# A new order for every engine of a fused window-attention and rational-MLP kernel, with three output tiles

## The chip, the cores and the metric

The kernel runs on one core of a Trainium2 chip. The metric is the device time of one execution in microseconds (us); smaller is better. The five engines are named as in the profile: PE (TensorE, matrix products), DVE (VectorE), ACT (ScalarE), POOL (GpSimd, here mostly the issuer of loads) and SP (SyncE, the issuer of transposing transfers and stores). PEld is PE's weight load.

## The reference

A causal attention with a window of 128 positions and 4 sink positions, followed by an MLP whose activation is a rational function.

```python
scores = scale * np.matmul(q, k.transpose(0, 1, 3, 2))     # B, H, S, D = 4, 8, 768, 64
keep = is_sink | in_window                                  # 4 sinks, window 128
a = softmax of scores where keep
attn = np.matmul(a, v)
x = attn as (3072, 512)
h = x @ w_in                                                # 512 -> 2048
P = a[0] + a[1]*h + a[2]*h**2 + a[3]*h**3
Q = 1.0 + abs(b[0])*abs(h) + abs(b[1])*h**2
return (P / (Q + 1e-06)) @ w_out                            # 2048 -> 512
```

## The kernel before

The 3,072 rows are cut into 12 steps of 256 rows, three steps to a batch. A step s goes through these pieces, whose names are those of the kernel's table of work:

- loads of K, Q and V. K and Q of steps 0 to 3 are turned by PE (`turn_k0`, `turn_q0`, `turn_kc`, `turn_qc`) and copied out of PSUM by DVE or ACT (`place_kc`, `place_qc`); K and Q of later steps are turned by SP's transposing transfers (`turn_k`, `turn_q`). V of steps 0 to 2 is rearranged by PE (`turn_vc`) and copied out (`place_vc`).
- `scores` (4 per step, PE), `exps` (4 per step, ACT), `attend` (2 per step, PE), then on DVE a reciprocal of the row sums (`rec`, line 854) and the scaled copy `norm` (line 860) into the tile x_n.
- `turn_x` and `placed_x`: x is turned by PE and copied to xblk by DVE or ACT in steps 0 to 4, and turned by SP's transfers in steps 5 to 11.
- `gemm1` (4 per step, PE, line 910) and `copy_in` (ACT, line 917) give hb.
- The rational function, on tiles of 4,096 columns: `and` (absolute value, L931), a square (`sqa` on ACT L924, `sqd` on DVE L926), `den` (L935), `even` (L940), `odd` (L944), `odd_h` (L948), `num` (L951) on DVE; `ln` (L954) and `exp` (L959) on ACT, which form the reciprocal of the denominator; `gate` (L964) on DVE gives g. Step 0 is cut into four parts of 1,024 columns, the last step into parts of 1,280, 1,280, 1,024 and 512 columns.
- `gemm2` (PE, line 974), `copy_out` (ACT, line 990) into an output tile o_t, and `store` (SP).

The sinks' part of V has a path of its own at the start: the coefficients a and b and four rows of V arrive by small transfers, DVE splits and casts them (L627, L630, L533), PE spreads them over the partitions, and DVE writes v_sink (L555, `spread_vs`). `attend` needs v_sink.

The order is written out by hand as a list of piece numbers, ORDER. The kernel walks it once and emits each piece; every engine then runs its own pieces in the order of the list, in order, each waiting for what it needs. A negative number is a filler: matmuls on a constant tile `warm` (line 728) that feed nothing. A table ENGINE says which of DVE and ACT does some 30 copies, and a table BANK gives each product one of four pairs of PSUM banks (ps_h, ps_o, ps_m, ps_s); a pair is free again when the piece that empties it is done. POOL's copies of one element (`hold`, L507) read x_n or hb of a step, and so keep the loads behind them in POOL's queue back until that step's part is written.

```python
names = list(work)
for n in ORDER:
    if n < 0:
        spin(-n)
    elif work[names[n]].run:
        work[names[n]].run()
```

Of the kernel before, what the change touches and what calls it, by code (L numbers as in the profile page):

```python
# [1429 lines left out]
```

## Time and profile before

| | before |
|---|---|
| time, median of 3 runs | 232.76 us (232.26 to 233.08) |
| the profiled execution | 232.42 us, of which the span of its instructions is 230.7 us |
| PE busy | 215.9 us (94% of the span) |
| DVE busy | 211.1 us (91%) |
| ACT busy | 207.0 us (90%) |
| POOL busy | 97.3 us (42%) |
| bytes moved by DMA | 26.98 MB |

Busy time is the time in which an engine worked on an instruction; the rest of the span it waited. The span leaves out 1.72 us of the profiled execution that lie around the instructions. PE's busy time includes the fillers.

### The profile page before, as it was taken

What the parts mean: (1) busy time and instruction counts of PE and PEld (TensorE: products, weight loads), DVE (VectorE), ACT (ScalarE), POOL (GpSimd) and SP (SyncE); (2) the same over time, 40 slices, a digit from 0 to 9 for tenths busy, and PEclk for the clock granted to TensorE, in tenths of its full rate; (3) what the DMA queues carried; (4) which work ended last, traced back from release to release, by engine and by line L of the source; (5) the groups of instructions that cost most, each with busy time, mean ns of one, the idle gap of its engine ahead of it and who ended that gap; (6) DMA issues with size and microseconds to landing.
All of it is one profiled execution on the core that took longest, in us unless ns stands there. A gap on an engine that the chain in (4) does not pass through costs nothing.

```text
span 230.7 us, 7350 instructions
## 1 busy us (share of the span) xinstructions
PE 215.9 (94%) x3249; PEld 147.0 (64%) x3271; DVE 211.1 (91%) x251; ACT 207.0 (90%) x177; POOL 97.3 (42%) x126
## 2 busy tenths in 40 slices
PE   8768999989999999999999999999999999999992
PEld 2546777778747667667677577758856875544441
DVE  3595699879999999999999999999999999999991
ACT  2757889989997999999999999999999999799961
POOL 8914756967559499988199800000000000000000
PEclk9999999999999999999999999999999999999999
DMA  6999999999999999999969998230050200400152
GB/s 182 199 191 199 197 144 103 135 117 121 205 176 141 130 106 150 172 122 124 196 155 133 109 148 162 47 71 0 3 139 3 48 0 0 182 4 0 49 224 91
DMA packets 95237, 26.98 MB, mean 117 GB/s; under 512 B 85862, under 2 KB 92262, under 8 KB 95206
## 3 DMA queue, kind: packets, MB, share of 16 engines
q0 software_dynamic: 65024, 12.98, 90.4%
q1 hardware_dynamic: 28942, 12.75, 29.8%
q10 hardware_dynamic: 1240, 0.79, 1.1%
q8 instruction: 25, 0.41, 0.8%
q14 instruction: 6, 0.05, 0.1%
HBM read 27.30 MB, written 6.29 MB: 146 GB/s over the span
## 4 chain that ended last, share of the span: by engine, by line
PE 69%; DMA 19%; POOL 3%; DVE 3%; issue 2%; ACT 2%; SPq 0%; DVEq 0%; ACTq 0%
PE ps_s L974 13%; PE ps_h L974 11%; PE ps_o L910 9%; PE ps_m L974 9%; PE ps_m L910 7%; DMA w_out_sb<-in_moe_w_out_dram 6%; PE ps_s L910 5%; PE ps_h L910 5%; DMA stage_v<-in_v_dram 4%; DMA k_bf<-in_k_dram 3%; DMA stage_a<-in_k_dram 2%; POOL v L465 2%; DMA ab_row<-in_moe_a_dram 2%; PE ps_o L846 2%; DMA q_bf<-in_q_dram 1%
## 5 line engine op out<-in xcount | busy, mean ns | idle before, releaser
L910 PEld LDWEIGHTS <-w_in_sb 128*128 128x128 bf16 x768 | 73.8, 98 | 13.0 <-issue 1.2
L974 PEld LDWEIGHTS <-g 128*128 128x128 bf16 x386 | 36.4, 98 | 41.6 <-issue 1.4
L954 ACT ACTIVATE lnq<-den 128x4096 f32<-128x4096 bf16 (+3 forms) x18 | 44.6, 2482 | 1.5 <-DVE den L935 1.4
L959 ACT ACTIVATE den<-lnq 128x4096 bf16<-128x4096 f32 (+3 forms) x18 | 44.5, 2484 | 0.2
L465 POOL DMA_DIRECT2D v<-in_v_dram x48 | 35.0, 746 | 3.6 <-DMA w_out_sb<-in_moe_w_out_dram 1.5
L910 PE MATMUL ps_o<-xblk,w_in_sb 128*128 128x256 bf16 x304 | 36.3, 273 | 0.0
L974 PE MATMUL ps_s<-w_out_sb,g 128*128 128x512 bf16 x136 | 32.3, 379 | 0.8 <-issue 0.5
L974 PE MATMUL ps_h<-w_out_sb,g 128*128 128x512 bf16 x121 | 28.6, 379 | 0.9 <-issue 0.5
L964 DVE TENSOR_TENSOR g<-num,den 128x4096 bf16<-128x4096 bf16 (+3 forms) x18 | 28.3, 1572 | 0.3
L935 DVE TENSOR_TENSOR den<-den,sq 128x4096 bf16<-128x4096 bf16 (+3 forms) x18 | 28.3, 1570 | 0.2
L951 DVE TENSOR_TENSOR num<-num,sq 128x4096 bf16<-128x4096 bf16 (+3 forms) x18 | 28.3, 1572 | 0.1
L948 DVE TENSOR_TENSOR sq<-sq,hb 128x4096 bf16<-128x4096 bf16 (+3 forms) x18 | 28.2, 1569 | 0.1
L910 PE MATMUL ps_m<-xblk,w_in_sb 128*128 128x256 bf16 x208 | 24.9, 273 | 0.5 <-DMA w_in_sb<-in_moe_w_in_dram 0.5
L974 PE MATMUL ps_m<-w_out_sb,g 128*128 128x512 bf16 x90 | 21.6, 379 | 0.6 <-issue 0.5
L917 ACT ACTIVATE hb<-ps_o 128x1024 bf16<-128x1024 f32 x19 | 19.5, 1029 | 2.1 <-PE ps_o L910 1.9
L924 ACT ACTIVATE sq<-hb 128x1024 bf16<-128x1024 bf16 (+3 forms) x15 | 20.0, 1341 | 0.1
L427 POOL DMA_DIRECT2D q_bf<-in_q_dram x15 | 16.7, 1111 | 6.0 <-DMA w_out_sb<-in_moe_w_out_dram 2.6
L910 PE MATMUL ps_s<-xblk,w_in_sb 128*128 128x256 bf16 x160 | 19.1, 273 | 0.0
L940 DVE TENSOR_SCALAR num<-sq,acoef 128x4096 bf16<-128x4096 bf16 (+3 forms) x18 | 18.3, 1023 | 0.3
L944 DVE TENSOR_SCALAR sq<-sq,acoef 128x4096 bf16<-128x4096 bf16 (+3 forms) x18 | 18.4, 1021 | 0.3
L507 POOL COPY seen<-x_n 1x1 bf16<-1x1 bf16 x8 | 9.7, 1225 | 17.4 <-DVE x_n L860 17.4
L926 DVE TENSOR_TENSOR sq<-hb 128x2048 bf16<-128x2048 bf16 (+2 forms) x13 | 16.8, 1295 | 0.1
(154 smaller groups left out, 321.5 us busy)
## 6 DMA issues: line engine op xcount, KB each, us to landing
out_dram<-o_t SPq DMA_DIRECT2D x11, 512.0 KB, 3.6
w_in_sb<-in_moe_w_in_dram POOLq DMA_DIRECT2D x4, 512.0 KB, 10.8
k_bf<-in_k_dram POOLq DMA_DIRECT2D x16, 128.0 KB, 6.6
w_out_sb<-in_moe_w_out_dram POOLq DMA_DIRECT2D x4, 512.0 KB, 11.7
q_bf<-in_q_dram POOLq DMA_DIRECT2D x15, 128.0 KB, 5.4
v<-in_v_dram POOLq DMA_DIRECT2D x24, 64.0 KB, 6.3
stage_v<-in_v_dram POOLq DMA_DIRECT2D x3, 256.0 KB, 9.6
v<-in_v_dram POOLq DMA_DIRECT2D x24, 32.0 KB, 5.7
```

Source lines behind the costliest of these rows:

```text
L465: nc.gpsimd.dma_start(out=v_fix[b % 2][half(r), g * NHF:(g + steps) * NHF, hl, 0:D], in_=v[b, h, g * TS:(g + steps) * TS, :].rearrange("(j ...
L910: nc.tensor.matmul(ps[:, n, :], lhsT=w_in_all[:, c, fc * P:(fc + 1) * P], rhs=xblk[m][:, c, :], start=(c == 0), stop=(c == NDMC - 1))
L917: nc.scalar.activation(out=hb[m][:, j * GW:(j + 1) * GW], in_=ps_h.pop((m, j)).rearrange("p n c -> p (n c)"), func=AF.Copy)
L924: nc.scalar.activation(out=sq[m][:, c], in_=hb[m][:, c], func=AF.Square)
L935: nc.vector.tensor_tensor(out=den[m][:, c], in0=den[m][:, c], in1=sq[m][:, c], op=ALU.add)
L944: nc.vector.tensor_scalar(out=sq[m][:, c], in0=sq[m][:, c], scalar1=a3, scalar2=a1, op0=ALU.mult, op1=ALU.add)
L948: nc.vector.tensor_tensor(out=sq[m][:, c], in0=sq[m][:, c], in1=hb[m][:, c], op=ALU.mult)
L951: nc.vector.tensor_tensor(out=num[m][:, c], in0=num[m][:, c], in1=sq[m][:, c], op=ALU.add)
L954: nc.scalar.activation(out=lnq_fix[:, c], in_=den[m][:, c], func=AF.Ln, scale=qsc_reg, bias=1.000001)
L959: nc.scalar.activation(out=den[m][:, c], in_=lnq_fix[:, c], func=AF.Exp, scale=-1.0)
L964: nc.vector.tensor_tensor(out=g_of[m][:, c], in0=num[m][:, c], in1=den[m][:, c], op=ALU.mult)
L974: nc.tensor.matmul(ps_out[own][:, tt, cols], lhsT=g_of[m][:, co:co + P], rhs=w_out_all[:, fc, cols], start=(fc == 0), stop=(fc == NFFC - 1 ...
```

## The change

The list ORDER is replaced by another one, and with it the tables ENGINE and BANK. No piece is added or taken away, except that a filler in the middle of the list (211: five matmuls) is gone and the one at the start becomes longer by one matmul of 512 columns (154 becomes 258). The output tiles o_t are three instead of two, and `copy_out` of step m waits for the store of step m-3 instead of m-2. The staging tile of the sinks' rows of V, stage_s, becomes a part of the staging tile stage_b. The short description of the change also names K of step 1 as first load; in POOL's queue the first three loads are, before and after, V of step 0, Q of step 1 and K of step 1. The next two change places (K of step 2 now ahead of Q of step 3).

In ENGINE eight copies go from ACT to DVE, and ten from DVE to ACT: `cast_q0` 1, both `cast_k0`, `place_k0` 0, `k_sink` 0 and 2, `place_vc` 0, `place_kc` 3, `placed_x` 2,0 and 4,1 to ACT; `cast_q0` 0, `place_k0` 1, `place_qc` 0,1 and 3,0, `k_sink` 1 and 3, `place_vc` 2 and `placed_x` 0,0 to DVE.

```diff
 ORDER = [
-    118, 2, 3, 0, -154, 108, 107, 129, 109, 117, 4, 119, 113, 116, 120, 121, 122, 1, 125, 143,
...
+    118, -258, 2, 3, 0, 108, 107, 109, 5, 119, 113, 4, 117, 120, 121, 122, 15, 1, 125, 143, 144,
...
-    ENGINE = {('cast_q0', 1): 'DVE',
-               ('place_kc', 3, None): 'DVE',
+    ENGINE = {('cast_q0', 1): 'ACT',
+               ('place_kc', 3, None): 'ACT',
...
-               ('place_vc', 0): 'DVE',
...
+               ('place_vc', 0): 'ACT',
...
-    BANK = {('attend', 0, 0): 'ps_s',
+    BANK = {('attend', 0, 0): 'ps_m',
...
-    o_sb = ctx.enter_context(tc.tile_pool(name="o_sb", bufs=2))
+    o_sb = ctx.enter_context(tc.tile_pool(name="o_sb", bufs=3))
...
-    stage_s = const_pool.tile([SR, B, D], FP32, name="stage_s")
+    stage_s = stage_b[0:SR, NQ0 * H * D:NQ0 * H * D + B * D].rearrange("p (b d) -> p b d", b=B)
...
-                      ends + [("store", m - 2, 0) if m >= 2 else None],
+                      ends + [("store", m - 3, 0) if m >= 3 else None],
...
```

What the new list does to the rows of an engine is shown at three places on DVE. The first is DVE's start, from the last sinks (v_sink, three rows) to the first instruction of the rational function (L931). qT, kT and xblk are the turned Q, K and x. Before:

```order
L555 TENSOR_TENSOR v_sink<-ps_o,ind 128x8x64 x3
L854 RECIPROCAL rec<-ps_s 128x8
L860 SCALAR_TENSOR_TENSOR x_n<-ps_s,ratio,rec 128x512
L679 COPY xblk<-ps_s 128x2x256
L679 COPY qT_101<-ps_m 128x4x128
L854 RECIPROCAL rec<-ps_h 128x8
L860 SCALAR_TENSOR_TENSOR x_n<-ps_h,ratio,rec 128x512
L370 MEMSET k_sink_104 128x80
L931 TENSOR_SCALAR den<-hb 128x512
```

And in the change, from the second `norm` of step 0 to the same instruction:

```order
L860 SCALAR_TENSOR_TENSOR x_n<-ps_s,ratio,rec 128x512
L679 COPY qT_102<-ps_o 128x2x384
L679 COPY xblk<-ps_s 128x2x256
L679 COPY xblk<-ps_o 128x2x256
L606 COPY cpow<-ratio 128x1
L607 TENSOR_TENSOR qsc<-bpos,ratio 128x1
L608 TENSOR_SCALAR cpow<-cpow,ratio 128x2
L610 TENSOR_TENSOR acoef<-ab_bc,cpow 128x4
L679 COPY qT_101<-ps_h 128x4x128
L931 TENSOR_SCALAR den<-hb 128x512
```

Half of step 3's Q (qT_102, 768 columns) and both halves of step 0's x are now DVE's, and L931 stands ahead of the first `norm` of step 1 instead of behind it.

The second place is DVE at the attention of step 3, whose two `rec` and `norm` stand together. Before:

```order
L860 SCALAR_TENSOR_TENSOR x_n<-ps_m,ratio,rec 128x512
L948 TENSOR_TENSOR sq<-sq,hb 128x1024
L745 TENSOR_TENSOR e_1_94<-e_1_94,sink_edge 128x4
L679 COPY xblk<-ps_m 128x4x128
L948 TENSOR_TENSOR sq<-sq,hb 128x1024
L854 RECIPROCAL rec<-ps_h 128x8
L854 RECIPROCAL rec<-ps_m 128x8
L860 SCALAR_TENSOR_TENSOR x_n<-ps_h,ratio,rec 128x512
L860 SCALAR_TENSOR_TENSOR x_n<-ps_m,ratio,rec 128x512
```

The change, from the same `norm` of step 2 on:

```order
L860 SCALAR_TENSOR_TENSOR x_n<-ps_m,ratio,rec 128x512
L948 TENSOR_TENSOR sq<-sq,hb 128x1024
L944 TENSOR_SCALAR sq<-sq,acoef 128x1024
L948 TENSOR_TENSOR sq<-sq,hb 128x1024
L951 TENSOR_TENSOR num<-num,sq 128x1024
L679 COPY xblk<-ps_h 128x4x128
L964 TENSOR_TENSOR g<-num,den 128x1024
L854 RECIPROCAL rec<-ps_o 128x8
L854 RECIPROCAL rec<-ps_s 128x8
L860 SCALAR_TENSOR_TENSOR x_n<-ps_s,ratio,rec 128x512
```

Ahead of the two `rec` there are now more pieces of step 0's rational function (`num`, `gate`), and one copy to xblk of step 2 instead of two, the other being ACT's.

The third place is DVE at the attention of step 5. Before, its two `rec` (ps_m and ps_h) stand behind `odd` and `odd_h` of step 2:

```order
L944 TENSOR_SCALAR sq<-sq,acoef 128x4096
L931 TENSOR_SCALAR den<-hb 128x2048
L854 RECIPROCAL rec<-ps_o 128x8
L860 SCALAR_TENSOR_TENSOR x_n<-ps_o,ratio,rec 128x512
L948 TENSOR_TENSOR sq<-sq,hb 128x4096
L854 RECIPROCAL rec<-ps_m 128x8
L679 COPY xblk<-ps_o 128x4x128
L854 RECIPROCAL rec<-ps_h 128x8
```

In the change both stand ahead of these two (the `rec` and `norm` of step 4, ps_o, are further up):

```order
L940 TENSOR_SCALAR num<-sq,acoef 128x4096
L931 TENSOR_SCALAR den<-hb 128x2048
L854 RECIPROCAL rec<-ps_h 128x8
L854 RECIPROCAL rec<-ps_s 128x8
L944 TENSOR_SCALAR sq<-sq,acoef 128x4096
L860 SCALAR_TENSOR_TENSOR x_n<-ps_h,ratio,rec 128x512
L948 TENSOR_TENSOR sq<-sq,hb 128x4096
L860 SCALAR_TENSOR_TENSOR x_n<-ps_s,ratio,rec 128x512
```

The two `rec` of step 5 moved up past `odd` (L944) and `odd_h` (L948) of step 2.

## Rows read from the trace of the kernel before

**Rows 1.** The page: busy time, then busy tenths and clock in 40 slices.

```profile
PE 215.9 (94%) x3249; PEld 147.0 (64%) x3271; DVE 211.1 (91%) x251; ACT 207.0 (90%) x177; POOL 97.3 (42%) x126
...
DVE  3595699879999999999999999999999999999991
...
PEclk9999999999999999999999999999999999999999
```

**Rows 2.** Waits of DVE: us in total, times, longest us.

```profile
DVE ab_part L627 <- DMA ab_row<-in_moe_a_dram: 1.5, 1, 1.5
...
DVE rec L854 <- PE ps_o L846: 0.4, 1, 0.4
```

**Rows 3.** Busy us of PE, PEld, DVE, ACT, POOL in three stretches, then granted clock.

```profile
10.00:15.00 5.00, 3.09 (x95) 2.29 (x84) 3.71 (x10) 3.31 (x5) 2.58 (x4) 1.00 1.73 186
...
40.00:50.00 10.00, 9.15 (x249) 7.59 (x247) 8.08 (x18) 9.23 (x11) 9.37 (x16) 1.00 2.12 116
...
190.00:200.00 10.00, 9.95 (x62) 5.90 (x62) 10.00 (x6) 9.40 (x7) 0.00 (x0) 1.00 0.08 32
```

**Rows 4.** DVE in order of time at the end: start us, us, what.

```profile
225.15 0.42 DVE L964 TENSOR_TENSOR g<-num,den 128x512 bf16<-128x512 bf16 x1
227.18 0.43 DVE L679 COPY o_t<-ps_o 128x256 f32<-128x256 f32 x1 [1.60 <-ACT o_t L677]
```

**Rows 5.** Groups of DVE's copies by shape: count, busy us, mean ns, idle before.

```profile
L679 DVE COPY kT<-ps_m 128x1024 bf16<-128x1024 bf16 x1 | 1.2, 1225 | 0.2 <-PE ps_m L661 0.2
...
L679 DVE CAST early<-stage_a 128x512 bf16<-128x512 f32 x2 | 1.0, 484 | 0.4 <-DMA stage_a<-in_k_dram 0.4
...
L679 DVE COPY xblk<-ps_m 128x512 bf16<-128x512 bf16 x2 | 0.8, 424 | 0.4 <-PE ps_m L885 0.2
...
L679 DVE COPY kT<-ps_m 128x512 bf16<-128x512 bf16 x1 | 0.7, 671 | 0.0
```

**Rows 6.** DVE in order of time, 0 to 45 us.

```profile
12.13 1.21 DVE L679 CAST v<-ps_o 128x1024 bf16<-128x1024 f32 x1
...
33.13 0.68 DVE L951 TENSOR_TENSOR num<-num,sq 128x1024 bf16<-128x1024 bf16 x1
```

**Rows 7.** PE in order of time, 0 to 45 us.

```profile
1.13 5.42 PE L728 MATMUL ps_h<-warm 128*128 128x512 bf16 x15 [1.13 <-DVE warm L1099]
...
13.39 0.64 PE L661 MATMUL ps_o<-ident,stage_d 128*64 128x128 bf16 x16 [1.18 <-DVE v L679]
...
16.56 0.77 PE L728 MATMUL ps_o<-warm 128*128 128x512 bf16 x5
...
21.74 1.92 PE L910 MATMUL ps_o<-xblk,w_in_sb 128*128 128x256 bf16 x16
...
27.97 0.77 PE L661 MATMUL ps_m<-ident,stage_v 128*64 128x128 bf16 x16 [0.45 <-DMA stage_v<-in_k_dram]
...
30.50 1.92 PE L910 MATMUL ps_m<-xblk,w_in_sb 128*128 128x256 bf16 x16 [0.53 <-DMA w_in_sb<-in_moe_w_in_dram]
...
38.88 1.92 PE L910 MATMUL ps_o<-xblk,w_in_sb 128*128 128x256 bf16 x16
```

**Rows 8.** DVE in order of time, 40 to 85 us.

```profile
42.06 0.42 DVE L679 COPY xblk<-ps_h 128x512 bf16<-128x512 bf16 x1 [0.69 <-PE ps_h L885]
...
48.67 0.21 DVE L854 RECIPROCAL rec<-ps_h 128x8 f32<-128x8 f32 x1 [0.78 <-PE ps_h L846]
49.19 0.21 DVE L854 RECIPROCAL rec<-ps_m 128x8 f32<-128x8 f32 x1 [0.31 <-PE ps_m L846]
...
80.78 0.20 DVE L854 RECIPROCAL rec<-ps_m 128x8 f32<-128x8 f32 x1
```

**Rows 9.** PE in order of time, 71 to 80 us: last attention products of step 5.

```profile
78.34 0.55 PE L846 MATMUL ps_h<-v,e 64*64 64x65 bf16 x24
```

**Rows 10.** The tile w_out_sb: its loads on POOL, and their time to landing.

```profile
L517 POOL DMA_DIRECT2D w_out_sb<-in_moe_w_out_dram x4: 747/748/768, 48.6 to 53.8; - x4
...
DMA to landing us min/median/max: 11.0/11.7/13.7
```

More of the change, by code (lines that the diff above doesn't have):

```diff
@@ L120 @@
     PE_MASK = tuple(range(12))
-    ENGINE = {('cast_q0', 1): 'DVE',
-               ('place_kc', 3, None): 'DVE',
+    ENGINE = {('cast_q0', 1): 'ACT',
+               ('place_kc', 3, None): 'ACT',
                ('place_qc', 0, 0): 'ACT',
-               ('place_qc', 0, 1): 'ACT',
-               ('k_sink', 0): 'DVE',
+               ('place_qc', 0, 1): 'DVE',
+               ('k_sink', 0): 'ACT',
                ('place_qc', 1, None): 'DVE',
                ('place_qc', 2, None): 'DVE',
-               ('place_qc', 3, 0): 'ACT',
-               ('place_vc', 0): 'DVE',
-               ('placed_x', 0, 0): 'ACT',
+               ('place_qc', 3, 0): 'DVE',
+               ('place_vc', 0): 'ACT',
+               ('placed_x', 0, 0): 'DVE',
                ('placed_x', 0, 1): 'DVE',
@@ L133 @@
                ('placed_x', 1, 1): 'DVE',
-               ('placed_x', 2, 0): 'DVE',
+               ('placed_x', 2, 0): 'ACT',
                ('placed_x', 2, 1): 'DVE',
@@ L137 @@
                ('placed_x', 4, 0): 'ACT',
-               ('placed_x', 4, 1): 'DVE',
+               ('placed_x', 4, 1): 'ACT',
                ('place_vc', 1): 'ACT',
-               ('place_vc', 2): 'ACT',
-               ('cast_k0', 0): 'DVE',
-               ('place_k0', 0): 'DVE',
-               ('cast_k0', 1): 'DVE',
-               ('place_k0', 1): 'ACT',
-               ('cast_q0', 0): 'ACT',
+               ('place_vc', 2): 'DVE',
+               ('cast_k0', 0): 'ACT',
+               ('place_k0', 0): 'ACT',
+               ('cast_k0', 1): 'ACT',
+               ('place_k0', 1): 'DVE',
+               ('cast_q0', 0): 'DVE',
                ('place_kc', 1, None): 'ACT',
@@ L148 @@
                ('place_qc', 3, 1): 'ACT',
-               ('k_sink', 1): 'ACT',
+               ('k_sink', 1): 'DVE',
                ('placed_x', 3, 0): 'DVE',
-               ('k_sink', 2): 'DVE',
-               ('k_sink', 3): 'ACT'}
-    BANK = {('attend', 0, 0): 'ps_s',
+               ('k_sink', 2): 'ACT',
+               ('k_sink', 3): 'DVE'}
+    BANK = {('attend', 0, 0): 'ps_m',
              ('attend', 0, 1): 'ps_s',
-             ('attend', 1, 0): 'ps_h',
-             ('attend', 1, 1): 'ps_s',
+             ('attend', 1, 0): 'ps_m',
+             ('attend', 1, 1): 'ps_m',
              ('attend', 2, 0): 'ps_m',
-             ('attend', 2, 1): 'ps_h',
-             ('attend', 3, 0): 'ps_h',
-             ('attend', 3, 1): 'ps_m',
+             ('attend', 2, 1): 'ps_o',
+             ('attend', 3, 0): 'ps_s',
+             ('attend', 3, 1): 'ps_o',
              ('attend', 4, 0): 'ps_m',
              ('attend', 4, 1): 'ps_o',
-             ('attend', 5, 0): 'ps_m',
+             ('attend', 5, 0): 'ps_s',
              ('attend', 5, 1): 'ps_h',
@@ L199 @@
              ('gemm1', 5, 2): 'ps_o',
-             ('gemm1', 5, 3): 'ps_h',
-             ('gemm1', 6, 0): 'ps_m',
-             ('gemm1', 6, 1): 'ps_o',
+             ('gemm1', 5, 3): 'ps_m',
+             ('gemm1', 6, 0): 'ps_o',
+             ('gemm1', 6, 1): 'ps_m',
              ('gemm1', 6, 2): 'ps_s',
@@ L205 @@
              ('gemm1', 7, 0): 'ps_m',
-             ('gemm1', 7, 1): 'ps_m',
-             ('gemm1', 7, 2): 'ps_o',
-             ('gemm1', 7, 3): 'ps_s',
-             ('gemm1', 8, 0): 'ps_s',
+             ('gemm1', 7, 1): 'ps_o',
+             ('gemm1', 7, 2): 'ps_s',
+             ('gemm1', 7, 3): 'ps_o',
+             ('gemm1', 8, 0): 'ps_m',
              ('gemm1', 8, 1): 'ps_s',
@@ L212 @@
              ('gemm1', 8, 3): 'ps_m',
-             ('gemm1', 9, 0): 'ps_o',
-             ('gemm1', 9, 1): 'ps_h',
+             ('gemm1', 9, 0): 'ps_h',
+             ('gemm1', 9, 1): 'ps_o',
              ('gemm1', 9, 2): 'ps_o',
              ('gemm1', 9, 3): 'ps_m',
-             ('gemm1', 10, 0): 'ps_h',
-             ('gemm1', 10, 1): 'ps_o',
+             ('gemm1', 10, 0): 'ps_o',
+             ('gemm1', 10, 1): 'ps_h',
              ('gemm1', 10, 2): 'ps_s',
-             ('gemm1', 10, 3): 'ps_h',
-             ('gemm1', 11, 0): 'ps_m',
-             ('gemm1', 11, 1): 'ps_h',
-             ('gemm1', 11, 2): 'ps_o',
+             ('gemm1', 10, 3): 'ps_m',
+             ('gemm1', 11, 0): 'ps_s',
+             ('gemm1', 11, 1): 'ps_m',
+             ('gemm1', 11, 2): 'ps_s',
              ('gemm1', 11, 3): 'ps_o',
              ('gemm2', 0, 0, 0): 'ps_h',
-             ('gemm2', 1, 0, 0): 'ps_s',
+             ('gemm2', 1, 0, 0): 'ps_o',
              ('gemm2', 2, 0, 0): 'ps_s',
@@ L231 @@
              ('gemm2', 6, 0, 0): 'ps_m',
-             ('gemm2', 7, 0, 0): 'ps_s',
-             ('gemm2', 8, 0, 0): 'ps_m',
-             ('gemm2', 9, 0, 0): 'ps_s',
-             ('gemm2', 10, 0, 0): 'ps_h',
-             ('gemm2', 11, 0, 0): 'ps_s',
-             ('gemm2', 11, 1, 0): 'ps_o',
+             ('gemm2', 7, 0, 0): 'ps_o',
+             ('gemm2', 8, 0, 0): 'ps_h',
+             ('gemm2', 9, 0, 0): 'ps_m',
+             ('gemm2', 10, 0, 0): 'ps_o',
+             ('gemm2', 11, 0, 0): 'ps_h',
+             ('gemm2', 11, 1, 0): 'ps_m',
              ('scores', 0, 0): 'ps_h',
-             ('scores', 0, 1): 'ps_s',
+             ('scores', 0, 1): 'ps_m',
              ('scores', 0, 2): 'ps_s',
@@ L259 @@
              ('scores', 5, 1): 'ps_o',
-             ('scores', 5, 2): 'ps_o',
-             ('scores', 5, 3): 'ps_m',
+             ('scores', 5, 2): 'ps_m',
+             ('scores', 5, 3): 'ps_s',
              ('scores', 6, 0): 'ps_m',
@@ L264 @@
              ('scores', 6, 2): 'ps_h',
-             ('scores', 6, 3): 'ps_h',
+             ('scores', 6, 3): 'ps_m',
              ('scores', 7, 0): 'ps_s',
@@ L268 @@
              ('scores', 7, 2): 'ps_m',
-             ('scores', 7, 3): 'ps_h',
-             ('scores', 8, 0): 'ps_s',
-             ('scores', 8, 1): 'ps_h',
-             ('scores', 8, 2): 'ps_m',
-             ('scores', 8, 3): 'ps_o',
-             ('scores', 9, 0): 'ps_s',
-             ('scores', 9, 1): 'ps_s',
-             ('scores', 9, 2): 'ps_o',
+             ('scores', 7, 3): 'ps_o',
+             ('scores', 8, 0): 'ps_m',
+             ('scores', 8, 1): 'ps_o',
+             ('scores', 8, 2): 'ps_s',
+             ('scores', 8, 3): 'ps_s',
+             ('scores', 9, 0): 'ps_o',
+             ('scores', 9, 1): 'ps_m',
+             ('scores', 9, 2): 'ps_h',
              ('scores', 9, 3): 'ps_o',
@@ L279 @@
              ('scores', 10, 1): 'ps_o',
-             ('scores', 10, 2): 'ps_o',
-             ('scores', 10, 3): 'ps_m',
-             ('scores', 11, 0): 'ps_s',
+             ('scores', 10, 2): 'ps_m',
+             ('scores', 10, 3): 'ps_s',
+             ('scores', 11, 0): 'ps_o',
              ('scores', 11, 1): 'ps_h',
-             ('scores', 11, 2): 'ps_h',
-             ('scores', 11, 3): 'ps_s',
+             ('scores', 11, 2): 'ps_s',
+             ('scores', 11, 3): 'ps_h',
              ('turn_k0', 0): 'ps_m',
@@ L1386 @@
     piece(("copy_out", LAST, 2), "ACT", 0.35, 0, lambda: copy_out(LAST, 2),
-          [("gemm2", LAST, 1, parts(LAST) - 1), ("store", LAST - 2, 0)])
+          [("gemm2", LAST, 1, parts(LAST) - 1), ("store", LAST - 3, 0)])
     piece(("store", LAST, 2), "ACT", 0.4, 0, lambda: store(LAST, 2), [("copy_out", LAST, 2)],
```

74 lines of the change are left out of this document (37 added, 37 removed), and 82 rows, old and new, of the table ORDER.

## The prediction

> **What bounds the kernel now.** I read the page's busy line and slices first [rows 1]. PE, DVE and ACT each work 90 to 94% of the span, and from the sixth slice on DVE's digits are 7 to 9 up to the last: no engine has much to give back except at the start. PE's 94% contains filler, so I asked next which engine the end hangs on. DVE's timeline ends with the last `gate` at 225.15 + 0.42 = 225.57 us; what follows (the last products, three copies, the stores) is a tail of 5.1 us to the end of the span at 230.7, in which DVE only waits 1.60 us for a small copy [rows 4]. Nothing in the change shortens that tail. Up to 225.57 DVE works 211.1 - 0.4 = 210.7 us [rows 1, 4], so it waits 14.9 us. The stretch table says where: 10.00 busy of 10.00 at 190 to 200 us, but 8.08 at 40 to 50 and 3.71 of 5 at 10 to 15 [rows 3]. So I treat the end as
>
> end = DVE's work + DVE's waits + 5.1 us of tail,
>
> and ask of the change what it does to the first two. PE and ACT are nearly as full, so this holds only as long as both stay ahead of DVE.
>
> **The work that changes hands.** Ten copies leave DVE, eight come to it. Equal kinds cancel: a cast of Q, half of `place_k0`, two `k_sink`, and `place_vc` 0 against `place_vc` 2. Left over, leaving: `place_kc` 3 at 1.225, two casts of K at 0.484, two copies to xblk at 0.424; together 3.04 us [rows 5]. Coming: one copy to xblk at 0.424 and two copies of turned Q with 768 columns, which DVE does nowhere in before. Their price lies between the copies of kT with 512 and 1,024 columns, 0.671 and 1.225 [rows 5]; between these by columns it is 0.95, which I take, since all three write with the same stride. Coming: 0.424 + 1.90 = 2.32. DVE's work changes by **-0.7** us (-1.3 to -0.15 at the two bounds). ACT gets about as much more, hidden as long as ACT runs ahead. PE loses the filler of 0.77 us at 16.56 [rows 7], which stood in a wait, and gains one filler matmul ahead of its first real work, some 0.4 us by the 5.42 us of the fifteen at the start [rows 7]; the first copy of Q waits for ACT's casts of K anyway, so it costs nothing. The third output tile is priced at nothing, both ways: no wait of DVE, and none that I saw of ACT's `copy_out`, ends with a store. The moved staging tile adds no wait.
>
> **The start.** In before, DVE waits 1.5 us for the coefficients, then spends 1.21 us on `place_vc` 0 (at 12.13) before the sinks, which also makes PE wait 1.18 at 13.39 [rows 2, 6, 7]. The coefficients arrive no earlier in the change. `place_vc` 0 is now on ACT, so the first sinks can be written at about 12.4 instead of 13.3. But the first `attend` now also waits until DVE has emptied the bank of Q of step 1 (about 14.8), and `place_qc` 3,0 stands ahead of both copies to xblk. Laid row by row with before's start-to-start times, both `norm` of step 0 end at 18.8, xblk is full at 20.6, and the first gemm1 starts at 21.05 (21.74 before [rows 7]) with the last `scores` of step 1 already done. K of step 3 has the same 3,616 KB ahead of and in it in the load queue as before, so it lands at 28.0 again [rows 7]. DVE then ends `num` of step 0's first part at 32.75 instead of 33.73, the next row's start behind 33.13 [rows 6]: 1.0 earlier, but it has 1.3 less work behind it by then, so it has waited **0.3 us more**. The bounds: no less waiting than 1.0 below before's (if K of step 3 came when the queue let it), and 1.3 above it (if the head gained nothing at all).
>
> **The waits between 40 and 50 us.** DVE waits 0.69, 0.78 and 0.31 us for PE here [rows 8], 1.78 together. PE gets earlier. After K of step 3 it has only to turn it and do one `attend` and one `scores` before the third gemm1; the other `scores` and Q went ahead of it, and the second half of w_in is loaded in an order that removes the wait of 0.53. So that gemm1 starts near 29.2 instead of 30.50, and the one of 38.88 near 36.6 to 37 [rows 7]. `scores` of step 4 moved behind the `attend` of step 3, which then end near 45.7, where before DVE started their `rec` at 48.67 and 49.19 [rows 8]. DVE has `num` and `gate` to do first and comes there at 45.7 to 46.0. **I take all three waits as gone, -1.8 us**; the margin is about zero, so the bound on the other side is that they all stay. Later, only one wait of 0.4 is left in before [rows 2], and the stretches near the end show DVE full [rows 3]; I change nothing there (bounds: the 0.4 gone, or a new wait, below).
>
> **Sum.** -0.7 + 0.3 - 1.8 = -2.2 us. The profiled execution took 232.42, so it gives 230.2; the median of the runs shown lies 0.34 above that execution, which gives 230.56. I say **230.5 us**. Its own range is 229.3 to 231.9 (the bounds of the copies of 768 columns, of the start on the good side and half of the three waits).
>
> **Rivals.**
>
> *The weights come late: no change.* The second load of w_out stands in POOL's queue behind the `hold` on x_n of step 3, that is behind that step's last `norm`, near 49.4 in the change; before, the loads of w_out were issued from 48.6 on and took 11.0 to 13.7 us to land [rows 10]. With those, it would land at 60.6 to 63.3, and gemm2 of step 0 wants it near 59.7. DVE's next product of PE (`rec` of step 4, second half, wanted at 65.3, ready at 64.2) has 1.1 us of slack, so DVE would wait 0 to 2.5 us and the whole gain could go: about 232.8. Against it: in the change fewer loads are in flight in front of it, so it should land faster.
>
> *`rec` of step 5 stands too early: slower.* Before, DVE reaches the `rec` at 80.78, 1.9 us after its product is done (78.34 + 0.55) [rows 8, 9]. In the change both `rec` stand ahead of `odd` and `odd_h` of step 2. By my chain DVE comes there near 74.5 and PE's second product ends near 74.7. If PE had kept none of its lead, it would end at 78.9: DVE would wait 4.4, and 4.4 - 2.2 gives 2.2 us slower, 234.8. It decides from 2.9 us of wait (0.7 slower). What speaks against it is that PE must then lose almost 3 of its some 4 us of lead in products that had no waits in before.
>
> *PE's clock falls: slower.* The granted clock reads 1.00 in all slices, the level of 2.4 GHz, also at 10 to 15 us where PE is busy 3.09 of 5 [rows 1, 3]. The change takes out the filler at 16.56 and leaves PE waits of about 1 us at 14 and 16. If these dropped PE to the level of 1.2 GHz, about 4.2 us of PE's work on the way to the first gemm1 would take twice as long: 4.2 - 2.2 gives 2.0 slower, 234.5; it decides from 2.9 of the 4.2. Before has a wait of 1.18 at 13.39 with no drop behind it [rows 7], so I give this little. The Trainium skill, TensorE: Matmul & The Clock Gate, section "Why this matters for your kernels", bears on this: it warns that idle gaps between bursts of matmuls bring the half-rate clock back. By that rule the change could end 2.0 us slower, as just worked out; the trace of before bears it out only so far as its gap of 1.18 us cost no clock.
>
> *The change doesn't do what it says: no change.* K of step 1 is not the first load, and no wait on a store existed for the third tile to remove. If the new list is only another of the same worth, the time is 232.8.
>
> **Chances.** Forecast 0.62, late weights 0.16, early `rec` 0.13, clock 0.03, same worth 0.06. About 0.3% (0.7 us) is what a measurement of this kernel can tell from no change. A part of the late weights (0.04) still ends below -0.7: faster 0.66; same 0.18, the rest of late weights and same worth; slower 0.16. To leave no more than 2 in 10 out, the range reaches from the good bounds, 229.2, to the late weights and the weak half of the early `rec`, 233.3.
>
> **What the changed profile would show.** DVE's gate ends near 223.4 instead of 225.57. Its busy time falls to about 210.4. Waits for PE at L854 and L679 between 40 and 50 us are gone. The third gemm1 starts near 29, the waits in front of L661 for K of step 3 stay. If the weights are late, L974 waits for w_out at 60 us and L854 behind it. If `rec` is early, L854 waits near 75 us. If the clock fell, a slice of its row is below 9. The forecast is wrong above all if PE or ACT, with 1 to 2 us less room than DVE needs, make new waits somewhere after 80 us, where I did not follow the new order row by row.

## The result, and the profile after

The change makes the kernel slower: 236.09 us (median of 4 runs, 234.51 to 237.26) against 232.51 for the kernel before (231.92 to 233.08), ratio 1.0144, 95% interval 1.0102 to 1.0187. The forecast was 230.5, with a range to 233.3. The profiled execution took 235.04 us, its span is 233.3. The ratios use the runs in each kernel's faster state alone and lie close to those of the means, so they can differ from the ratio of the medians.

The page of the changed kernel: busy time, then busy tenths and clock in 40 slices, then one DMA queue (packets, MB, share).

```profile
PE 219.3 (94%) x3267; PEld 146.5 (63%) x3267; DVE 211.5 (91%) x249; ACT 208.3 (89%) x179; POOL 94.1 (40%) x126
...
DVE  4586687899999999999999999999999999999991
...
PEclk9999997999999999999999999999999999999998
...
q8 instruction: 25, 0.41, 0.8%
```

Against [rows 1], DVE's digits are lower in slices 3, 6 and 7 (8, 8 and 7 for 9 each; slices 6 and 7 are 29 to 41 us), and 9 from the ninth slice to the last but one. The clock has one slice of 7. DVE's timeline has the end:

```profile
227.72 0.42 DVE L964 TENSOR_TENSOR g<-num,den 128x512 bf16<-128x512 bf16 x1
229.75 0.42 DVE L679 COPY o_t<-ps_m 128x256 f32<-128x256 f32 x1 [1.60 <-ACT o_t L677]
```

The last `gate` ends at 228.14 instead of 225.57 [rows 4], and the tail is the same 5.1 us, so the equation of the prediction can be filled in: 2.57 us more of DVE's work and waits. Where they lie is read by cutting the time at two points that both orders have, the end of the first `num` of step 0 and the end of the last `norm` of step 3. Stretches of the kernel before (length, then busy us and count of PE, PEld, DVE, ACT, POOL, then granted clock, DMA share, GB/s):

```profile
0.00:33.81 33.81, 27.08 (x594) 19.35 (x595) 23.05 (x70) 22.92 (x30) 20.56 (x38) 1.00 1.48 189
33.81:50.68 16.87, 15.73 (x393) 12.87 (x391) 14.73 (x32) 15.78 (x18) 13.43 (x22) 1.00 2.15 111
50.68:225.57 174.89, 171.98 (x2261) 114.28 (x2281) 172.86 (x151) 167.45 (x129) 63.28 (x67) 1.00 1.11 104
```

and of the change:

```profile
0.00:33.95 33.95, 27.04 (x593) 19.41 (x594) 21.99 (x67) 24.48 (x31) 22.01 (x41) 1.00 1.50 190
33.95:54.17 20.22, 18.43 (x399) 14.58 (x396) 16.72 (x35) 16.89 (x20) 11.09 (x19) 0.92 2.56 105
54.17:228.15 173.98, 172.72 (x2280) 112.02 (x2272) 172.34 (x148) 166.06 (x128) 60.97 (x68) 1.00 1.02 103
```

Length less DVE's busy time is DVE's waiting: 10.76, 2.14 and 2.03 us before, 11.96, 3.50 and 1.64 after. So DVE waits 1.2 us more at the start, 1.4 more in the middle (the forecast had 1.8 less) and 0.4 less behind; its work is 0.4 more. PE's timeline shows what DVE waited for:

```profile
16.78 0.38 PE L846 MATMUL ps_m<-v,e 64*64 64x65 bf16 x18 [0.73 <-issue]
...
29.23 0.61 PE L661 MATMUL ps_o<-ident,stage_v 128*64 128x128 bf16 x15 [1.09 <-issue]
...
30.54 1.92 PE L910 MATMUL ps_s<-xblk,w_in_sb 128*128 128x256 bf16 x16
...
36.66 0.41 PE L494 MATMUL ps_s<-stage_v,sel 64*64 64x256 bf16 x7 [1.79 <-issue]
...
38.02 3.17 PE L910 MATMUL ps_m<-xblk,w_in_sb 128*128 128x256 bf16 x16
```

PE stops three times, 3.61 us in all, each time inside a piece whose operands are there: the stop at 36.66 comes after nine of the 16 products of `turn_vc` 2, the one at 29.23 after one of the 16 of `turn_kc` 3. "Issue" says that no event in the profile released it. The kernel before has two such stops in its first 60 us, of 0.29 and 0.53 us (at 35.24 and 59.37); the first, at the same record of PE as the stop at 36.66:

```profile
35.24 0.51 PE L494 MATMUL ps_s<-stage_v,sel 64*64 64x256 bf16 x10 [0.29 <-issue]
```

The slow `gemm1` at 38.02 stands in the slice with the lower clock. In order of time DVE then waits for PE here:

```profile
37.11 1.23 DVE L679 CAST v<-ps_s 128x1024 bf16<-128x1024 f32 x1 [1.55 <-PE ps_s L494]
...
41.99 0.21 DVE L854 RECIPROCAL rec<-ps_o 128x8 f32<-128x8 f32 x1 [1.32 <-PE ps_o L846]
...
49.44 0.42 DVE L679 COPY xblk<-ps_h 128x512 bf16<-128x512 bf16 x1 [0.47 <-PE ps_h L885]
```

The places of the stops have a pattern that counting shows. Stretches of the changed kernel that end at the three stops, columns as above:

```profile
0.00:16.77 16.77, 12.15 (x223) 7.20 (x224) 10.36 (x39) 10.84 (x15) 13.50 (x28) 1.00 1.34 192
16.77:29.20 12.43, 10.17 (x255) 8.00 (x255) 7.90 (x21) 9.57 (x12) 5.90 (x7) 1.00 1.43 198
29.20:36.65 7.45, 5.64 (x128) 4.74 (x127) 5.30 (x13) 6.18 (x7) 4.28 (x9) 1.00 2.58 150
```

Matmuls and weight loads together are 447, then 510, then 255. With the one or two other instructions of PE that this view leaves out they are 449, 512 and 256 in the trace: the stops stand 256 instructions apart, or twice that. The queue named "instruction" on the page carries 25 packets and 0.41 MB, so 16 KB each, one for each 256 of PE's some 6,550 instructions; in the trace a packet goes with each boundary, and at the three stops PE goes on 1.5, 1.4 and 2.2 us after a packet's end.

That is my theory: **PE receives its instructions in blocks of 256, one block ahead; while the DMA engines are full of loads the next block comes late, and where a block is worked off fast PE runs dry.** The Trainium skill, Runtime: NRT & Kernel Launch, section "Instruction fetch mechanics", states such blocks of 256 instructions and 16 KiB, fetched by DMA, and calls crossing a boundary mostly hidden. The count agrees, and 22 of the 25 boundaries are crossed without such a stop; these three are not.

The pace of the packets bears on why the kernel before hardly stops. Up to 34 us they begin 6.1 to 6.7 us apart in both kernels (at 13.84, 19.97, 26.24 and 32.45 us before, 14.32, 20.81, 26.89 and 33.55 in the change). PE of the kernel before went through the four blocks from record 193 to 1217 in 23.9 us, about 6 each, and so asked for little more than that pace; the change asks sooner.

Rivals: loads of V and K that come late without the profile naming them, the clock, and an order that is worth no more in itself.

### The profile page after: what moved, and what is told of

It reads as the page before. It is cut to its first block, busy times and chain, and to the rows that moved or that the text cites. A ratio compares the mean times of both kernels' runs of the same rounds, so it can differ in the third digit from the quotient of the medians.

```text
span 233.3 us, 7371 instructions
## 1 busy us (share of the span) xinstructions
PE 219.3 (94%) x3267; PEld 146.5 (63%) x3267; DVE 211.5 (91%) x249; ACT 208.3 (89%) x179; POOL 94.1 (40%) x126
## 5 line engine op out<-in xcount | busy, mean ns | idle before, releaser
L974 PEld LDWEIGHTS <-g 128*128 128x128 bf16 x386 | 36.4, 98 | 41.6 <-DVE g L964 2.0
L465 POOL DMA_DIRECT2D v<-in_v_dram x48 | 34.2, 731 | 4.7 <-DVE rec L854 2.1
L974 PE MATMUL ps_h<-w_out_sb,g 128*128 128x512 bf16 x144 | 34.0, 380 | 0.2 <-DVE g L964 0.2
L948 DVE TENSOR_TENSOR sq<-sq,hb 128x4096 bf16<-128x4096 bf16 (+3 forms) x18 | 28.4, 1576 | 0.2
L910 PE MATMUL ps_m<-xblk,w_in_sb 128*128 128x256 bf16 x224 | 28.0, 281 | 0.0
L910 PE MATMUL ps_s<-xblk,w_in_sb 128*128 128x256 bf16 x224 | 26.8, 273 | 0.0
L974 PE MATMUL ps_m<-w_out_sb,g 128*128 128x512 bf16 (+1 forms) x114 | 26.4, 376 | 0.0
L910 PE MATMUL ps_o<-xblk,w_in_sb 128*128 128x256 bf16 x208 | 24.9, 273 | 0.9 <-DVE x_n L860 0.8
L974 PE MATMUL ps_o<-w_out_sb,g 128*128 128x512 bf16 x96 | 21.7, 379 | 0.0
L458 POOL DMA_DIRECT2D k_bf<-in_k_dram x16 | 15.2, 953 | 10.1 <-DMA kT<-k_bf 3.8
L944 DVE TENSOR_SCALAR sq<-sq,acoef 128x4096 bf16<-128x4096 bf16 (+3 forms) x18 | 18.3, 1016 | 0.2
L427 POOL DMA_DIRECT2D q_bf<-in_q_dram x15 | 15.8, 1060 | 3.4 <-DMA w_in_sb<-in_moe_w_in_dram 3.0
L846 PEld LDWEIGHTS <-e 64*64 64x64 bf16 x1216 | 13.4, 107 | 5.1 <-issue 3.7
## 6 DMA issues: line engine op xcount, KB each, us to landing
w_in_sb<-in_moe_w_in_dram POOLq DMA_DIRECT2D x4, 512.0 KB, 12.4
```

The lines of the kernel that those rows point to most:

```text
L465: nc.gpsimd.dma_start(out=v_fix[b % 2][half(r), g * NHF:(g + steps) * NHF, hl, 0:D], in_=v[b, h, g * TS:(g + steps) * TS, :].rearrange("(j ...
L910: nc.tensor.matmul(ps[:, n, :], lhsT=w_in_all[:, c, fc * P:(fc + 1) * P], rhs=xblk[m][:, c, :], start=(c == 0), stop=(c == NDMC - 1))
L948: nc.vector.tensor_tensor(out=sq[m][:, c], in0=sq[m][:, c], in1=hb[m][:, c], op=ALU.mult)
L974: nc.tensor.matmul(ps_out[own][:, tt, cols], lhsT=g_of[m][:, co:co + P], rhs=w_out_all[:, fc, cols], start=(fc == 0), stop=(fc == NFFC - 1 ...
```

## The experiments

The kernels below were run in groups, each beside the kernel before, whose time was 232.68 us (the first four kernels below), 232.99 (the change once more, three loads of w_in left out, four loads later), 232.76 (w_in cut to one load, w_out moved) and 232.07 (both cuts, one wait of the kernel before). Ratios are to these. Records are PE's instructions, counted from the start.

**Do the stops follow the count or the place?** The opening filler in narrow pieces, 56 products of 128 columns for 14 of 512 and 2 of 128 (256 columns fewer in all): 80 more PE instructions ahead of the program.

```diff
-    118, -258, 2, 3, 0, ...
+    118, -256, 2, 3, 0, ...
-        wide = cols.shape[1] // P
+        wide = 1 if n == 56 else cols.shape[1] // P
```

> The changed kernel with the opening filler cut into 56 products of 128 columns instead of 14 of 512 and 2 of 128: the same columns, but 80 more PE instructions ahead of the first real one, and nothing else. Theory one (PE gets its instructions in blocks of 256, and stops at the end of a block until about 1.4 us after the 16 KB transfer that brings the next one): the stops stay at PE's records 449, 961 and 1217 counted from the start, which are now 80 records earlier in the program, so the stop of 1.8 us in front of the tenth product of turn_vc of step 2 and the one of 1.1 us behind the first product of turn_kc of step 3 are gone from these places and stand elsewhere, also at blocks of 256; the time stays 233.5 to 238. Theory two (V of step 2 and K of step 3 come late): the stops stay in front of the same products. Time 235 to 236.

Measured: 235.31 us, ratio 1.0109 (1.0068 to 1.0149). The stretches up to its stops:

```profile
0.00:15.75 15.75, 11.01 (x223) 9.44 (x224) 8.97 (x38) 9.85 (x14) 12.74 (x27) 1.00 1.31 190
15.75:21.90 6.15, 4.00 (x127) 2.92 (x127) 5.47 (x13) 3.77 (x4) 3.39 (x5) 1.00 1.47 197
21.90:34.30 12.40, 10.71 (x256) 8.09 (x256) 6.28 (x15) 9.62 (x12) 4.76 (x6) 0.86 1.75 185
```

Again 447, then 254 and 512. In PE's timeline the last of them stands in the middle of a `gemm1`, five of whose 16 products had run:

```profile
34.31 1.36 PE L908 MATMUL ps_s<-xblk,w_in_sb 128*128 128x256 bf16 x11 [1.61 <-issue]
```

The instruction queue's packets are 26 instead of 25. The two pieces that had stopped, `turn_kc` 3 and `turn_vc` 2, run without a stop. Late V and K are out: the stops went with the count. That they moved and the time did not suggests that it is the rate that costs, not one place.

**Does the slow clock cost the time?** A filler in the stop.

```diff
-    ... ('turn_vc', 2) ...
+    ... -28, ('turn_vc', 2) ...
```

> The changed kernel with a filler of seven products of 512 columns (1.5 us at 2.4 GHz) right ahead of turn_vc of step 2, in the stretch from 34.4 us in which PE stops for 1.8 us. If the slow stretch of the clock at 37.2 to 40.6 us comes of that stop and costs time of its own, the granted clock stays at 2.4 GHz, the gemm1 behind it takes 1.92 us instead of 3.17 and the kernel is 1.0 to 1.7 us faster than the change, 233.5 to 235. If the stop itself is all that costs, the time stays 235 to 236. If the filler only adds work it is 1.5 us slower, 237.5.

Measured: 234.69 us, 1.0074 (1.0043 to 1.0104), against 235.00 and 1.0081 for the change run again (below): no difference, where 1.0 to 1.7 us had been expected if the clock cost time of its own. The clock stayed at 2.4 GHz at this place (in this execution it fell earlier, from 18.2 to 21.6 us) and the `gemm1` took its 1.92 us, but a stop came one block later:

```profile
37.71 1.92 PE L908 MATMUL ps_m<-xblk,w_in_sb 128*128 128x256 bf16 x16
40.18 1.27 PE L908 MATMUL ps_s<-xblk,w_in_sb 128*128 128x256 bf16 x10
42.63 0.83 PE L908 MATMUL ps_s<-xblk,w_in_sb 128*128 128x256 bf16 x6 [1.19 <-issue]
```

DVE's waits up to the end of step 3 were 14.99 us instead of 15.46: a small part of what was to be explained. Of the 26 runs of the kernel before in this group, 18 had a mean granted clock under 1.000; their median is 232.75, that of the other eight 232.34, so 0.4 us less. In the group with w_in cut the difference was 0.7 us (8 runs and 3), in the last group -0.2 (14 and 7). The clock is worth less than 1 us, not 2.6.

**Fewer loads under way at the same time.** The `hold` on x_n of step 0 back to its old place, ahead of the loads of K of step 3, w_in 3, V of step 2 and three others.

```diff
-    ('load_kc', 3) ... ('load_w_in', 3) ... ('load_k', 5, 0) ('load_vc', 2) ... ('norm', 0, 1) ... ('hold', 'x', 0)
+    ('norm', 0, 1) ('hold', 'x', 0) ('load_kc', 3) ('load_w_in', 3) ('load_k', 5, 0) ('load_vc', 2) ...
```

> The changed kernel with POOL's hold on x_n of step 0 put back to where the kernel before has it: right behind that step's norm, and the loads of K of step 3, the last quarter of w_in, K of steps 5 and 4, V of step 2 and a Q behind it, so that they are issued from 20 us on instead of from 13.3. Theory one with a rider (the transfer that brings PE's next 256 instructions starts late because many loads are under way): it starts 2.3 us behind the end of a block, as in the kernel before, instead of 3.5 to 4.3, the stops of 1.1 and 1.8 us shrink to 0.3 and 0.6, the clock stays up, 231.5 to 233.5. Without the rider (16 engines full are full either way) the stops stay and the time is 235 to 237. If K of step 3 or V of step 2 then land later than 28 and 33 us, PE waits for them and it is slower than the change.

Measured: 233.40 us, 1.0039 (1.0007 to 1.0070), about 1 us better than the change run again by the ratios, whose intervals just overlap. The time is in the range given for shorter ways of the blocks, but the blocks' ways were not shorter. In the trace the transfers of the next blocks still began 3.9 to 4.5 us behind the boundaries at 16.3, 23.2 and 29.4 us, with a stop of 1.53 at the last; the one at record 1217 was gone, and stops of 0.28 and 0.37 us came later. Issuing these loads later didn't shorten a block's way while the engines were full.

**The three output tiles alone,** in the kernel before.

```diff
-    o_sb = ctx.enter_context(tc.tile_pool(name="o_sb", bufs=2))
+    o_sb = ctx.enter_context(tc.tile_pool(name="o_sb", bufs=3))
...
-                      ends + [("store", m - 2, 0) if m >= 2 else None],
+                      ends + [("store", m - 3, 0) if m >= 3 else None],
```

> The kernel before with the three output tiles alone (copy_out waits for the store three steps back, and the sinks' staging tile is a part of another tile, which makes the room). By my account no wait hangs on a store, so the same as before within 0.3%: 232.1 to 233.2. If the order of the change needed the third tile or the third tile cost something, it would be seen here as a time over 233.5.

Measured: 232.87 us, 1.0008 (0.9981 to 1.0036): nothing, as the prediction had it.

**The change once more,** unedited.

> The changed kernel as it is, on the same chip as the other kernels of this call, to have its stops twice. If PE's stops at its records 449, 961 and 1217 belong to the kernel they come again, within half a us each, 234.5 to 237; if the first profile showed a mishap, they are gone and the time is that of the kernel before, 232.7.

Measured: 235.00 us, 1.0081 (1.0058 to 1.0103). Its stops come at the same counts, 0.71, 0.69 and 1.51 us. The change is 2.0 us slower here and was 3.6 by the medians of the result. The trace read above is of an execution of 235.04 us; what made two of the first four runs take 237 is not in it, and stays open.

**Three of four loads of w_in left out,** in both kernels.

```diff
     def load_w_in(j):
+        if j:
+            return
...
-            fc = j * GC + n
+            fc = n
```

> The changed kernel with three of the four loads of w_in left out (all gemm1 read the first quarter, so three quarters of the weights are left out of the result): 1,536 KB less to load before 33 us, and the same instructions on every computing engine. If PE's stops come from instruction blocks whose transfer waits behind the loads, the transfer starts 1 to 2 us after the block's start instead of 3.3 to 4.3 in the stretch where the loads are fewer (from about 20 us), the stops at records 961 and 1217 fall to below 0.4 us, and the kernel gains 2 to 4 us, 231 to 233.5. If the stops have a cause inside PE, they stay, and the gain is only what K of step 3 gains by landing earlier, at most 1 us.

> The kernel before with the same three loads of w_in left out, as the measure for the one above: its stops are 0.3 and 0.5 us, and its waits for w_in and K of step 3 0.5 each, so it can gain 0.5 to 1.5, 231 to 232.2. If my sum for the change was right but for the stops, the changed kernel is 1 to 2.5 us faster than this one when both load lightly; if the new order is worth nothing or less in itself, it is not faster than this one here either.

Measured: 232.05 us for the change (0.9970, 0.9937 to 1.0003) and 231.13 for the kernel before (0.9928, 0.9890 to 0.9966). The stop at record 1217 is gone from the change, and the transfer that follows record 961 began 1.2 us after it instead of 4.3; the stops at 449 (0.58) and 961 (0.94) stayed, where loads still filled the engines. The change gained 3.0 us, the kernel before 1.9. The new order was not the faster one here. Cut at the two points as above, the middle stretch has 0.17 us of DVE's waits in the change and 1.66 in the kernel before, and the start 12.62 and 9.75.

**w_in cut to one load of 128 KB,** in both kernels.

```diff
-        nc.gpsimd.dma_start(
-            out=w_in_all[:, :, f0:f1],
-            in_=moe_w_in[:, f0:f1].rearrange("(c p) f -> p c f", p=P))
+        nc.gpsimd.dma_start(out=w_in_all[:, 0, f0:f1], in_=moe_w_in[0:P, f0:f1])
...
-                nc.tensor.matmul(ps[:, n, :], lhsT=w_in_all[:, c, fc * P:(fc + 1) * P],
+                nc.tensor.matmul(ps[:, n, :], lhsT=w_in_all[:, 0, fc * P:(fc + 1) * P],
```

> The changed kernel with the loads of w_in cut to one of 128 KB (every gemm1 reads this one block, so most of the weights are left out of the result): 1,920 KB less in the first 33 us, the computing engines' instructions unchanged. If PE's stops are blocks of instructions waiting behind the loads of w_in, the one at record 449 (fetched at 14 us, when the loads are still full) may stay at 0.5 to 0.9, those at 961 and 1217 go, the transfers start under 2 us after the block's start from 20 us on, and the time falls to 229.5 to 231.5. If the stop of 1.16 at record 961, which stood with three loads left out, has another cause, it stays at about 1 us and the time stays at 232.

> The kernel before with the same loads cut. It has little left to gain against the one with three loads left out (231.1): 230.3 to 231.3. If the new order is better in itself, as my sum said, and only the supply of instructions spoils it, the changed kernel is here 0.5 to 1.5 us faster than this one; if it is not, the sum's start is wrong also without the stops.

Measured: 231.08 us for the change (0.9934, 0.9900 to 0.9969) and 231.74 for the kernel before (0.9935, 0.9897 to 0.9972), above the 230.3 to 231.3 expected of it. The medians differ by 0.66 us and the ratios by nothing, so the two are not told apart. The change's stretches, cut at the same two points:

```profile
0.00:33.68 33.68, 27.24 (x593) 19.46 (x594) 21.63 (x67) 24.47 (x31) 19.52 (x38) 1.00 1.43 156
33.68:50.52 16.84, 16.70 (x399) 13.95 (x396) 16.68 (x36) 16.50 (x20) 11.05 (x19) 1.00 1.94 81
50.52:224.16 173.64, 170.87 (x2258) 112.17 (x2279) 171.88 (x149) 166.13 (x128) 59.63 (x68) 1.00 0.99 103
```

In the middle stretch DVE waits 0.16 us instead of 3.50. But the kernel before, with the same cut, also waits less there, 0.63 us instead of 2.14 (its stretch):

```profile
34.30:49.42 15.12, 14.79 (x388) 12.37 (x386) 14.49 (x32) 14.97 (x18) 11.22 (x19) 1.00 2.65 107
```

The two `rec` of step 3, which the prediction put at 45.7 to 46.0 with no wait, come at 46.6 to 46.8 in DVE's timeline of the change, without a wait:

```profile
46.60 0.20 DVE L852 RECIPROCAL rec<-ps_o 128x8 f32<-128x8 f32 x1
46.80 0.21 DVE L852 RECIPROCAL rec<-ps_s 128x8 f32<-128x8 f32 x1
```

The stop at record 961 stayed (1.10 us), and with it a start with 12.05 us of DVE's waits (10.88 in the kernel before with the same cut).

**Four loads of steps 4 and 5 later,** behind the `hold` on x_n of step 1, nothing left out.

```diff
-    ('load_k', 5, 0) ... ('load_k', 4, 0) ('load_q', 11) ... ('load_k', 4, 1) ... ('hold', 'x', 1)
+    ('hold', 'x', 1) ('load_k', 4, 0) ('load_q', 11) ('load_k', 4, 1) ('load_k', 5, 0)
```

> The changed kernel with four loads of later steps (both of K of step 4, one of K of step 5, one of Q) put behind POOL's hold on x_n of step 1, so that they are issued from 32 us on instead of from 17.5 to 27: less is under way between 24 and 33 us, and V of step 2 lands by 30 instead of 32.7. By the theory of the blocks the stop at record 961 stays near 1 us, for until then as much is under way, and the one at 1217 shrinks from 1.8 to 0.5 or less: 0.5 to 1.5 us faster than the change. If the loads of K of step 4 then come late for its scores at 43.6, PE waits there for kT and the gain goes.

Measured: 233.45 us, 1.0027 (0.9998 to 1.0057), 1.5 better than the change run again. The stop at record 1217 is gone, but in the profiled run, the longest of the six (235.02 us), one at record 2241 has come, behind the loads of w_out (PE in order of time):

```profile
29.23 0.61 PE L659 MATMUL ps_o<-ident,stage_v 128*64 128x128 bf16 x15 [1.41 <-issue]
...
60.43 0.32 PE L844 MATMUL ps_m<-v,e 64*64 64x65 bf16 x16 [1.31 <-issue]
```

**Both cuts together:** w_in as one load of 128 KB, and the four loads later.

> The changed kernel with w_in cut to one load of 128 KB (most of the weights are left out of the result) and, besides, the four loads of later steps put behind the hold on x_n of step 1: until 32 us only what steps 0 to 3 need of Q, K and V is loaded. With the cut alone the stops at records 449 and 961 stayed at 0.4 and 1.1 us, with blocks that came 4.6 and 3.3 us after the one before was begun. If these two wait behind loads as well, they fall below 0.3 us, the first num ends by 33.0 instead of 33.7, and the time is 229.5 to 230.8, as my sum had it. If they stay, the supply has a delay of its own in this stretch that no load explains, and the time stays at 231.

Measured: 233.52 us, 1.0066 (1.0037 to 1.0095). The stop at record 961 is gone, and `turn_kc` 3 and `turn_vc` 2 run through:

```profile
28.45 0.64 PE L659 MATMUL ps_o<-ident,stage_v 128*64 128x128 bf16 x16 [0.23 <-ACT e L803]
...
33.61 0.63 PE L492 MATMUL ps_s<-stage_v,sel 64*64 64x256 bf16 x16
```

In the trace the transfers now began 0.0 us after and 0.7 us before PE passed the boundaries at 23.88 and 28.46. The stop at 449, when loads still filled the engines, stayed (0.66). So the supply is not slow by itself in this stretch. The time was not as expected: a stop of 1.43 at 59.5, again behind w_out, and a wait of 0.51 for V at 47 took the gain back. The first `num` ended at 33.37, not by 33.0.

**Can the loads of w_out be moved out of the way?** Three of the four to 39 to 50 us, on top of the four later loads (the edit shown); and, in the kernel before, two of them to behind the `hold` on x_n of step 1.

```diff
-    ('hold', 'h', 1) ... ('load_k', 5, 1) ... ('load_v', 4, 4) ... ('load_w_out', 0) ... ('load_w_out', 1) ('load_w_out', 3)
+    ('hold', 'h', 1) ('load_w_out', 0) ... ('load_k', 5, 1) ('load_w_out', 1) ... ('load_v', 4, 4) ('load_w_out', 3)
```

> The changed kernel with the four loads of later steps put back as in the run above of that kind, and three of the four loads of w_out moved up in POOL's queue, behind the hold on hb of step 1, K of step 5 and a V of step 4, so that they are under way between 39 and 50 us and not together at 53 to 57. The stop of 1.5 us at record 2241, whose block came 5.3 us late behind them, falls below 0.5, and the time is 231.5 to 232.8, at or below the kernel before; if V of steps 3 and 4 come late instead, attend waits for v and it stays at 233.5.

> The kernel before with two loads of w_out moved up in POOL's queue, behind the hold on x_n of step 1 and a load of K of step 6, from 49 to 51 us to about 42 to 45. The same order of every computing engine; the stop of 0.5 us at record 2241 and the wait of 0.3 us for w_out go: 0.3 to 0.8 us faster than the kernel before. If it delays V of step 4, PE waits for v: up to 1 us slower.

Measured: 242.05 us (1.0386, 1.0352 to 1.0421) and 240.18 us (1.0191, 1.0136 to 1.0245; the runs of the second spread from 235.26 to 242.61, and its profiled run is the longest). V came late; PE in the first kernel, then in the second:

```profile
65.71 0.55 PE L844 MATMUL ps_m<-v,e 64*64 64x65 bf16 x24 [6.36 <-DMA v<-in_v_dram]
...
65.19 0.37 PE L844 MATMUL ps_m<-v,e 64*64 64x65 bf16 x10 [4.47 <-DMA v<-in_v_dram]
```

What is put ahead in the queue of loads delays the rest of it.

**One wait of the kernel before.** K of step 5 and a V of step 6 behind the Q that PE waits for at 47.7.

```diff
-    ... ('load_v', 6, 7) ... ('load_k', 5, 1) ... ('load_q', 11) ...
+    ... ('load_q', 11) ('load_k', 5, 1) ('load_v', 6, 7) ...
```

> The kernel before with two loads that are used late (K of step 5, and a V of step 6) moved in POOL's queue behind the Q of steps 4 and 5. PE's wait of 0.74 us for qT at 47.7 falls to nothing, and with it the two waits of DVE at rec of step 3: 0.3 to 0.8 us faster than the kernel before, 231.9 to 232.5. If the wait for qT hangs on SP's queue of transposes and not on the loads, no change.

Measured: 232.55 us, 1.0056 (1.0030 to 1.0081): not faster, and slower by 0.2 to 0.6% (medians, ratio). The wait for qT is gone from the profile, and DVE waits 0.81 us in the middle stretch instead of 2.14. But a stop stands elsewhere, at record 1985, and behind the middle stretch DVE waits 3.16 us instead of 2.03:

```profile
51.50 0.27 PE L770 MATMUL ps_s<-qT,kT 64*64 64x192 bf16 x3 [1.33 <-issue]
```

No version here beats both kernels without leaving work out.

## Why the prediction was wrong

The prediction laid PE's pieces one behind the other at the duration that each had before, and asked only for operands and banks. The runs show a further limit, the supply of PE's instructions. In the change and its second run, the transfer for the next block begins 3.3 to 4.3 us after a PE that has stopped goes on; it takes about 1.0, and PE goes on 1.2 to 2.2 after its end. That is 5.5 to 7.5 us for 256 instructions; from stop to stop 512 took 12.4 us and 256 took 7.4. With the stops taken out of the trace, PE runs the four blocks between records 193 and 1217 in 5.1, 6.6, 4.7 and 5.5 us, 21.9 in all. The kernel before took 23.9. A chain that puts PE's pieces 0.7 to 2 us earlier than before, as mine did, needs the blocks faster than they came.

- **The waits between 40 and 50 us, -1.8:** the step that failed. Measured +1.4 in the stretch from the first `num` to the end of step 3. K of step 3 landed as said (first product of `turn_kc` 3 at 27.93), but the third `gemm1` came at 30.54, not 29.2, and the one expected at 36.6 to 37 at 38.02 and at half clock. With w_in cut to 128 KB the same stretch has 0.16 us of waits, as the chain had it. But like against like, the kernel before has 0.63 there with that cut, and with three loads left out it is 0.17 against 1.66. So where the blocks come in time the new order does remove these waits, which is worth 0.5 to 1.5 us by these four executions, less than the 1.8 of the sum; with all loads the supply took that away and more.
- **The start, +0.3:** measured +1.2. The first `gemm1` came at 21.50 (21.05 forecast) and the first `num` ended at 33.95 (32.75). The stop of 1.09 in `turn_kc` 3 is about that difference. With it gone (both cuts together) the first `num` ended at 33.37, so some 0.6 us of the term is not explained by it; a stop of 0.66 at record 449 and 3.4 us at the lower clock stood in that run. The prediction's own bound for this term was 1.3, but its range took the bound on the good side only.
- **The work that changes hands, -0.7:** measured +0.4. The copies of 768 columns took 0.952 us, as taken. What was not in the sum: the ten `even` and ten `odd` of 4,096 columns took 1.1 us more than before (last section). With w_in cut, DVE's work is 0.6 us less in the change than in the kernel before (210.19 against 210.75), so the count of copies was about right.
- **Behind 50 us, nothing:** measured -0.4.

Sum: 0.4 + 1.2 + 1.4 - 0.4 = 2.6 against -2.2 forecast.

The rivals. *Late weights:* no; the loads of w_out took 8.0 us at the median to land (11.7 before), and no wait of L974 for them is left. *Early `rec`:* no wait came of it, but by luck: PE's second product ended at 79.73, later than the 78.9 of the rival's worst case, and DVE itself was late and came to the pair at 79.53, not 74.5. *Clock:* a slice below 9, as named, but in the profiled execution not where the removed filler and the gaps of 14 to 16 us were. It followed the stop of 1.79 us. Between 30 and 50 us the granted clock was 0.86 and 0.97, which is 3.4 us at 1.2 GHz and made one `gemm1` take 3.17 us instead of 1.92. That bears out what the prediction cited of the Trainium skill, TensorE: Matmul & The Clock Gate, section "Why this matters for your kernels". In other executions the clock did fall for 3.4 us where the rival had it: from 17.4 us in the change run again, behind its stop of 0.71 us, and from 14.6 us in the kernel before with one wait moved, although the wait at 13.39 that the prediction leaned on had cost no clock in its trace. As the cause of the 2.6 us it is out: with the clock held behind the stop the ratio was 1.0074, without 1.0081. *Same worth:* this was the nearest. With w_in cut to one block the change measured 0.9934 and the kernel before 0.9935 of the same reference, so the deficit of 0.8% that the change had in its second run was gone with those loads; with three of them left out, half of it was left (0.9970 against 0.9928). Whether the new order is better by itself once the stops are gone stays open, since no run had all of them gone. The times given with two rivals, 234.8 and 234.5, are 0.2 below 232.76 plus their 2.2 and 2.0; nothing hangs on it.

What also stays open: why PE goes on 1.2 us after a transfer's end at one stop and 2.2 at another, and by what the loads hold the transfers up. That the DMA engines are busy is not enough: the page's DMA digits stay at 9 up to 140 us, but between 78 and 140 us the transfers of the change began from 0.2 us before to 3.0 us after their boundary, and no stop came there. That the stops cost the time is shown by cutting loads, which also lets data land earlier; no run removed the stops alone.
